# Folding the half sums of the exponentials for 14 pairs instead of 10, five of them with accumulating DMAs, and a drain behind every GpSimd addition

## The chip, the core and the metric

The kernel runs on one NeuronCore of a Trainium2 chip. The core has a matrix engine (TensorE, PE in the profile), VectorE (DVE), ScalarE (ACT), GpSimd (POOL), a queue engine that issues most of the DMAs (SyncE, SP), and 16 DMA engines that all the queues share. The metric is the device time of one launch in microseconds; the time before is the median of three runs.

## What is computed

The reference is an attention block followed by an MLP mixer, all in float32:

```python
B, H, S, D = 4, 8, 768, 64
mask = q_assign[:, :, :, None] == k_assign[:, :, None, :]   # nearest of 16 centroids
scores = np.where(mask, scale * q @ k.T, -1e9)
attn = np.exp(scores - max)
attn = attn / (attn.sum(-1) + 1e-9)
x = (attn @ v) laid out as (B, S, H*D)                      # 4 x 768 x 512
h = relu(x.T @ w_tok1) @ w_tok2                             # token mixing, 768 -> 256 -> 768
u = x + h.T
out = u + relu(u @ w_ch1) @ w_ch2                           # channel mixing, 512 -> 1536 -> 512
```

What the change touches is the row sum of the exponentials, `attn.sum(-1)`, which divides the product with `v`.

## The kernel before

**Stages.** The 32 heads are worked in 16 pairs (`NP`), `pair(m)` for m = 0 to 15. After them comes the token stage (`token1`, `token2`), then the channel stage, `channel1` and `channel2` for two groups of two batches each. The products of both MLP stages are done by a Strassen-like scheme with seven products instead of eight, so VectorE and GpSimd add and subtract operand blocks in between.

**A pair.** `scores(m)` makes the scores in 12 chunks on TensorE and ScalarE takes their exponential (L1193) into six buffers of 128 x 1536 floats, one for each block of 128 keys. `values(m, i)` multiplies block i with `v` (L1226), 16 matmuls a block. `add_up(m)` adds, on VectorE, the first three exponential buffers into `es[0]` (two additions) and the last three into `es[1]` (two additions); each is 128 x 1536. `sums(m)` multiplies them with a column of ones on TensorE, which sums over the partitions; it is issued one pair later, inside pair m+1, behind the first values block. `finish_x` transposes the result, takes the reciprocal and scales x.

**FOLD.** One character for each pair says how the two half sums are joined. With "-", `sums` runs TensorE over both `es` buffers, accumulating in PSUM. With "V", VectorE adds `es[0]` to `es[1]` first, and TensorE runs over `es[1]` alone. With "T", a DMA issued from GpSimd's queue adds `es[0]` to `es[1]` in SBUF while it moves it, and TensorE again runs over `es[1]` alone. The kernel before has "V" for pairs 1 to 10, "-" for pairs 0 and 11 to 15, and no "T".

```python
a, b = es[1], es[0]
if FOLD[m] == "V":
    tt(a.ap, a.ap, b.ap, ALU.add, 2 * S, a.k() + b.k(), a.k())
if FOLD[m] != "T":
    return
...
first = 0 if FOLD[m] == "-" else 1
for n in range(first, 2):
    mms(...)            # 4 matmuls of 384 columns, over es[n]
```

**Weight rounding.** Between these, VectorE rounds and recombines the MLP weights, in 31 pieces (`weight_round`, L1356 to L1374, five instructions a piece) with additions of 256 and 448 columns between them. The pieces start to be loaded at set times during the attention and are stored back to DRAM in the `wd` tensors.

**Order of the work.** The order on every engine but TensorE is made when the kernel is built: `Program.plan` is a list scheduler that knows a cost for each operation (the table `COST`, in us), latencies and due times, and puts each engine's instructions in the order that its model gives. The engines then run their queues strictly in that order and wait on semaphores. TensorE's order is the order in which the code issues the matmuls. A changed cost or operation can therefore move many instructions of VectorE, ScalarE, GpSimd and SyncE.

**Buffers.** There is one `es[0]` and one `es[1]`, used by every pair. VectorE cannot start `es[0]` of the next pair before whoever reads the old one is done.

**GpSimd.** It has 179 additions of 128 x 384 (`tt` with engine POOL, L883), all in the token and channel stages; most make the operand sums of the channel products, in two buffer sets that alternate from product to product.

Of the kernel before, what the change touches and what calls it, by code (L numbers as in the profile page):

```python
# [48 lines left out]
SUM_LO, SUM_HI = 1e-15, 1e15  # L49
GRAIN = 32  # L50
CHECK_AT = 532.0
FOLD = "-VVVVVVVVVV-----"

COST = {
    "ACT": (0.09, 0.00083),
    "ACT16": (-0.275, 0.001426),
    "JOIN16": (-0.165, 0.001426),
    "DVE": (0.075, 0.00104),
    "POOL": (0.12, 0.0023),
}  # L60
ISSUE = 0.63
BUS = 240e3
# [660 lines left out]
def kernel(  # L723
# [26 lines left out]
    nc = tc.nc  # L750
# [105 lines left out]
    def cost(kind, n):  # L856
        a, b = COST[kind]
        return a + b * n
# [22 lines left out]
    def tt(dst, a, b, op, n, rd, wr, engines=("DVE",)):  # L881
        def fn(e):
            (nc.vector if e == "DVE" else nc.gpsimd).tensor_tensor(out=dst, in0=a, in1=b, op=op)  # L883

        return g.add({e: cost(e, n) for e in engines}, fn, rd, wr)

# [184 lines left out]
    def route(m, bk):  # L1071
# [13 lines left out]
        def blocks(t):  # L1085
# [3 lines left out]
        vec(lambda: nc.vector.reduce_max(out=mxs.ap[:, 0:24], in_=blocks(a), axis=AX.X), 0.54,  # L1089
            a.k(), mxs.k())  # L1090
        tt(blocks(e), blocks(a), mxs.ap[:, 0:24].unsqueeze(2).to_broadcast([P, 24, C]),
           ALU.is_ge, HS, a.k() + mxs.k(), e.k())
        vec(lambda: nc.vector.transpose(out=o.ap, in_=e.ap), 0.56, e.k(), o.k())
# [107 lines left out]
    def add_up(m):  # L1201
        st = unit[m]
        for n in range(2):
            a = es[n]
            x, y, z = st[HJ * n : HJ * n + HJ]
            tt(a.ap, x.ap, y.ap, ALU.add, 2 * S, x.k() + y.k(), a.k())
            tt(a.ap, a.ap, z.ap, ALU.add, 2 * S, a.k() + z.k(), a.k())
# [6 lines that stand above are left out]
        def fn(e):  # L1214
            nc.gpsimd.dma_start(
                a.ap.rearrange("p h t -> p (h t)"), b.ap.rearrange("p h t -> p (h t)"),
                accum_op=ALU.add,
            )

        g.add({"POOL": 1.0}, fn, a.k() + b.k(), a.k(), (2.2 * 768 * 1024, 6144))  # L1220
# [30 lines left out]
    def sums(m, bk):  # L1251
        first = 0 if FOLD[m] == "-" else 1
        for n in range(first, 2):
            mms(
                [
                    (
                        ps[32 * gr : 32 * gr + 32, bk, 0:HS], ones.ap,
                        tokens(es[n].ap.rearrange("p h t -> p (h t)"), gr), n == first, n == 1,
                        (0, 32 * gr),
                    )  # L1260
                    for gr in range(4)
                ],
                0.645, es[n].k() + ones.k(), bank(bk), (P, 32),
            )
# [768 lines left out]
```

## Time and profile before

| | us |
|---|---|
| median of 3 runs | 793.61 (793.22 to 793.68) |
| profiled execution | 794.77 |
| its span | 793.0 |
| PE busy | 780.1 (98%) |
| VectorE busy | 677.5 (85%) |
| ScalarE busy | 461.2 (58%) |
| GpSimd busy | 190.2 (24%) |
| HBM traffic | 91.95 MB read, 28.61 MB written |

The span is the time from the first to the last instruction of the program; some 1.8 us of the profiled execution lie outside it. The granted TensorE clock was 0.999 of full speed. In the profile each float32 matmul is two records. The attention takes the span's first 329 us (the last matmul of L1226 starts at 329.0), the token stage runs to about 405, and the channel stage from there to 787.

### The profile page before, as it was taken

The numbers are of one execution on the slowest core, as the hardware profiler recorded it, in microseconds if no ns is written. First come the engines' busy times: TensorE is split into PE (matmuls) and PEld (weight loads), VectorE is DVE, ScalarE is ACT, GpSimd is POOL, SyncE is SP. The second block draws the span as 40 slices with busy tenths as digits, with TensorE's granted clock in tenths as the row PEclk, the third lists the DMA queues.
The fourth block names the chain that finished last, engine by engine and source line by source line (L and its number), as shares of the span: only waits on it lengthen the run. The fifth ranks groups of instructions, "written<-read, shape, count | busy, mean of one in ns | idle before, by whom it ended". The sixth has DMA issues, their size and how long they took to land.

```text
span 793.0 us, 15364 instructions
## 1 busy us (share of the span) xinstructions
PE 780.1 (98%) x5983; PEld 465.4 (59%) x5983; DVE 677.5 (85%) x876; ACT 461.2 (58%) x612; POOL 190.2 (24%) x185
## 2 busy tenths in 40 slices
PE   7999999999999999999999999999999999999997
PEld 6666666666666666544555555555555555555554
DVE  6869999999999999999999967899953567799964
ACT  4688898888898875599714367642245204400422
POOL 0000000000000000001264599700186379830000
PEclk9999999999999999999999999999999999999999
DMA  9576769777678953659858999975788844444767
GB/s 214 154 174 164 183 151 232 205 219 203 162 207 183 273 180 113 182 110 224 184 139 246 312 290 258 270 191 123 167 188 179 170 106 102 100 101 106 162 144 178
DMA packets 326576, 143.68 MB, mean 181 GB/s; under 512 B 260192, under 2 KB 322400, under 8 KB 326496
## 3 DMA queue, kind: packets, MB, share of 16 engines
q1 hardware_dynamic: 324128, 141.83, 71.4%
q8 instruction: 49, 0.80, 0.4%
q10 hardware_dynamic: 2368, 0.79, 0.4%
q14 instruction: 31, 0.25, 0.1%
HBM read 91.95 MB, written 28.61 MB: 152 GB/s over the span
## 4 chain that ended last, share of the span: by engine, by line
PE 88%; DVE 5%; ACT 3%; issue 2%; DMA 1%; SPq 0%; POOL 0%; DVEq 0%; POOLq 0%; ACTq 0%
PE ps L844 72%; PE ps L1226 16%; DVE arena L883 4%; ACT arena L873 2%; DMA wd<-arena 1%; ACT arena L1193 1%; DVE arena L865 0%; DVE arena L1360 0%; SPq L903 0%; DVE arena L1363 0%; ACT arena L863 0%; DVE arena L1366 0%; DVE arena L1356 0%; DVE arena L1280 0%; DVE arena L1273 0%
## 5 line engine op out<-in xcount | busy, mean ns | idle before, releaser
L844 PE MATMUL ps<-arena 128*128 128x384 f32 (+5 forms) x2735 | 642.4, 463 | 7.3 <-DVE arena L865 2.7
L844 PEld LDWEIGHTS ps<-arena 128*128 128x128 f32 (+1 forms) x2351 | 342.3, 185 | 252.8 <-issue 59.5
L883 DVE TENSOR_TENSOR arena<-arena 128x1536 f32<-128x1536 f32 (+6 forms) x350 | 370.2, 1079 | 10.5 <-PE ps L1226 2.3
L883 POOL TENSOR_TENSOR arena<-arena 128x384 f32<-128x384 f32 x179 | 189.5, 1094 | 510.8 <-DVE arena L883 379.4
L883 DVE TENSOR_TENSOR arena<-ps,arena 128x384 f32<-128x384 f32 (+3 forms) x227 | 189.6, 845 | 79.4 <-PE ps L844 75.4
L873 ACT COPY arena<-arena 128x768 uint16<-128x768 uint16 x221 | 189.4, 953 | 61.4 <-DMA arena<-arena 31.9
L1193 ACT ACTIVATE arena<-ps 128x768 f32<-128x768 f32 x192 | 150.6, 811 | 31.6 <-PE ps L844 29.9
L1226 PE MATMUL ps<-arena 128*32 128x192 f32 (+1 forms) x3248 | 144.7, 335 | 0.0
L1226 PEld LDWEIGHTS ps<-arena 128*32 128x32 f32 x3248 | 103.8, 110 | 44.0 <-issue 13.9
L863 ACT COPY arena<-ps 128x384 f32<-128x384 f32 (+2 forms) x41 | 29.5, 728 | 120.6 <-PE ps L844 120.4
L890 ACT ACTIVATE arena<-arena 128x1152 f32<-128x1152 f32 (+1 forms) x38 | 39.9, 1075 | 54.9 <-DVE arena L883 54.5
L1888 ACT ACTIVATE arena<-arena 128x768 f32<-128x768 f32 x40 | 38.7, 970 | 32.7 <-DMA arena<-in_moe_w_ch_dram 24.7
L844 PEld LDWEIGHTS <-arena 64*128 64x128 bf16 x384 | 19.3, 94 | 25.0 <-issue 0.6
L1360 DVE SCALAR_TENSOR_TENSOR arena<-arena 128x512 uint32<-128x512 uint32 (+1 forms) x31 | 20.6, 681 | 0.3
L1097 ACT ACTIVATE arena<-arena 128x384 bf16<-128x384 f32 x16 | 11.2, 703 | 16.1 <-issue 16.1
L1366 DVE SCALAR_TENSOR_TENSOR arena<-arena 128x512 f32<-128x512 uint32 (+1 forms) x31 | 20.2, 671 | 0.4
L1356 DVE TENSOR_SCALAR arena<-arena 128x512 uint32<-128x512 uint32 (+1 forms) x31 | 13.2, 435 | 5.8 <-DMA arena<-in_moe_w_tok_dram 5.8
L1273 DVE STREAM_TRANSPOSE arena<-ps 128x768 f32<-128x768 f32 x16 | 15.3, 955 | 0.0
L1363 DVE TENSOR_SCALAR arena<-arena 128x512 uint32<-128x512 uint32 (+1 forms) x31 | 14.4, 483 | 0.3
L865 DVE COPY arena<-ps 128x384 f32<-128x384 f32 (+3 forms) x12 | 8.0, 666 | 4.7 <-PE ps L844 4.6
L1088 DVE STREAM_TRANSPOSE arena<-ps 128x384 f32<-128x384 f32 x16 | 9.2, 575 | 3.1 <-PE ps L844 3.0
L1280 DVE STREAM_TRANSPOSE arena<-ps 128x384 f32<-128x384 f32 x16 | 9.3, 579 | 1.5 <-PE ps L1226 1.2
(58 smaller groups left out, 53.1 us busy)
## 6 DMA issues: line engine op xcount, KB each, us to landing
arena<-wd SPq DMA_DIRECT2D x196, 192.0 KB, 3.0
wd<-arena SPq DMA_DIRECT2D x84, 224.0 KB, 3.2
arena<-in_moe_w_ch_dram SPq DMA_DIRECT2D x96, 128.0 KB, 3.0
arena<-in_moe_w_ch_dram SPq DMA_DIRECT2D x16, 768.0 KB, 6.0
arena<-in_v_dram SPq DMA_DIRECT2D x16, 384.0 KB, 4.7
out_dram<-arena SPq DMA_DIRECT2D x14, 384.0 KB, 3.6
arena<-in_k_dram SPq DMA_DIRECT2D x13, 384.0 KB, 4.0
arena<-in_q_dram SPq DMA_DIRECT2D x13, 384.0 KB, 4.2
```

What stands on the lines that cost most here:

```text
L844: nc.tensor.matmul(dst, lhsT=lhsT, rhs=rhs, start=start, stop=stop, tile_position=pos, is_transpose=tr, skip_group_check=True,)
L863: nc.scalar.copy(out=dst, in_=src)
L873: nc.scalar.copy(out=dst, in_=src)
L883: (nc.vector if e == "DVE" else nc.gpsimd).tensor_tensor(out=dst, in0=a, in1=b, op=op)
L890: nc.scalar.activation(out=dst, in_=src, func=ACT.Relu)
L1193: lambda e, ex=ex, s=s, u=u: nc.scalar.activation(out=ex.ap[:, :, u * HS : (u + 1) * HS], in_=ps[:, 2 * s : 2 * s + 2, 0:HS], func=ACT.Exp ...
L1226: nc.tensor.matmul(dst, lhsT=lhsT, rhs=rhs, start=start, stop=stop, tile_position=pos, skip_group_check=True,)
L1273: lambda: nc.vector.transpose(out=x.ap[:, :, cols].rearrange("p j (c d) -> p c j d", d=32), in_=ps[:, 6:8, 0:HS],),
L1360: vec(lambda: nc.vector.scalar_tensor_tensor(out=TT, in0=hi, scalar=0xC0000000, in1=hh, op0=ALU.bitwise_and, op1=ALU.bitwise_or), 0.14 + 0 ...
L1363: vec(lambda: nc.vector.tensor_scalar(out=hh, in0=TT, scalar1=0xFF800000, scalar2=None, op0=ALU.bitwise_and), f, T.k(), h.k())
L1366: vec(lambda: nc.vector.scalar_tensor_tensor(out=ll, in0=lo, scalar=float(2.0**-52), in1=hh.bitcast(F32), op0=ALU.mult, op1=ALU.mult,), 0. ...
L1888: lambda e, i=i, func=func, bias=bias, n=n, hi=hi: nc.scalar.activation(out=hi, in_=hi, func=func, bias=bias, accum_out=wsum.ap[:, i, n : ...
```

## The change

Three edits. The string `FOLD` now folds pairs 1 to 14: VectorE does nine of them (1 to 5, 7, 9, 11, 13) and an accumulating DMA five (6, 8, 10, 12, 14). Every GpSimd addition is followed by a drain of GpSimd. And the scheduler's cost of a GpSimd addition gets 0.08 us more of fixed part.

```diff
-FOLD = "-VVVVVVVVVV-----"
+FOLD = "-VVVVVTVTVTVTVT-"
 COST = {
...
-    "POOL": (0.12, 0.0023),
+    "POOL": (0.2, 0.0023),
 }
...
     def tt(dst, a, b, op, n, rd, wr, engines=("DVE",)):
         def fn(e):
             (nc.vector if e == "DVE" else nc.gpsimd).tensor_tensor(out=dst, in0=a, in1=b, op=op)
+            if e == "POOL":
+                nc.gpsimd.drain()
```

The part of `add_up` that "T" reaches stood in the kernel before without being used:

```python
def fn(e):
    nc.gpsimd.dma_start(
        a.ap.rearrange("p h t -> p (h t)"), b.ap.rearrange("p h t -> p (h t)"),
        accum_op=ALU.add,
    )
g.add({"POOL": 1.0}, fn, a.k() + b.k(), a.k(), (2.2 * 768 * 1024, 6144))
```

Each such DMA moves 128 rows of 6144 bytes, 768 KB, from `es[0]` onto `es[1]`.

## The prediction

> **What bounds the kernel now.** The page first: the totals, the slices, the shares of the chain.
>
> ```profile
> PE 780.1 (98%) x5983; PEld 465.4 (59%) x5983; DVE 677.5 (85%) x876; ACT 461.2 (58%) x612; POOL 190.2 (24%) x185
> ...
> PE   7999999999999999999999999999999999999997
> ...
> DVE  6869999999999999999999967899953567799964
> ...
> PE 88%; DVE 5%; ACT 3%; issue 2%; DMA 1%; SPq 0%; POOL 0%; DVEq 0%; POOLq 0%; ACTq 0%
> ```
>
> TensorE sets the time nearly everywhere, so a matmul removed should be time removed. But VectorE is as full in the attention and in the token stage, so the next view is the chain of waits in order of time (start, duration, what).
>
> ```profile
> 230.87 9.89 PE ps L844 x72
> 240.76 5.98 PE ps L1226 x136
> 246.74 0.65 PE ps L844 x8
> 247.38 2.60 PE ps L1226 x64
> ...
> 299.88 9.23 PE ps L1226 x208
> ...
> 415.33 370.91 PE ps L844 x1154
> ```
>
> A pair is a scores block of 9.9 us and then values with sums, without a hole. The block at 240.76 holds a folded pair's sums: 200 records in 5.98 + 2.60 = 8.58 us. The one at 299.88 holds an unfolded pair's: 208 records in 9.23 us. Eight records more are 0.65 us. From 415 on the chain is TensorE alone. What lies between is seen in the busy time by stretch (PE, weight loads, VectorE, ScalarE, GpSimd, clock, DMA share, GB/s) and in TensorE's own timeline.
>
> ```profile
> 180.00:200.00 20.00, 20.00 (x288) 12.49 (x286) 19.23 (x26) 17.20 (x24) 0.00 (x0) 1.00 0.65 184
> 300.00:320.00 20.00, 20.00 (x308) 12.81 (x304) 19.68 (x28) 10.41 (x13) 0.00 (x0) 1.00 0.35 113
> 365.00:405.00 40.00, 39.33 (x115) 21.11 (x115) 38.59 (x78) 25.63 (x32) 11.83 (x12) 1.00 0.85 196
> 405.00:440.00 35.00, 34.64 (x108) 20.09 (x107) 33.08 (x38) 14.45 (x19) 19.86 (x18) 1.00 0.68 200
> 440.00:460.00 20.00, 20.00 (x64) 11.75 (x63) 17.08 (x19) 7.07 (x14) 12.08 (x13) 1.00 1.06 311
> ```
>
> ```profile
> 364.70 31.53 PE L844 MATMUL ps<-arena 128*128 128x384 f32 x91
> 396.73 18.24 PE L844 MATMUL ps<-arena 128*128 128x384 f32 x54 [0.50 <-DVE arena L883]
> 415.33 5.11 PE L844 MATMUL ps<-arena 128*128 128x384 f32 x15 [0.36 <-DVE arena L883]
> ```
>
> In the token stage VectorE is busy 38.59 of 40 us and TensorE waits for it: 91 records should take 91 x 0.3214 = 29.2 us (370.91 / 1154 is 0.3214), and took 31.53. So the end of the token stage is set by TensorE and VectorE together, and a gain of the attention reaches the end only if VectorE comes earlier too.
>
> **Part 1: matmuls removed.** Pairs 11 to 14 are folded anew. Each loses one pass of `sums`, 0.65 us by the two blocks above: 4 x 0.65 = 2.6 us, all on the path, since the blocks around it have no hole.
>
> **Part 2: VectorE's work.** Mean times of one instruction, by shape:
>
> ```profile
> L883 DVE TENSOR_TENSOR arena<-arena 128x1536 f32<-128x1536 f32 x90 | 156.4, 1747 | 5.4 <-PE ps L1226 2.3 <-ACT arena L1193 0.5 <-PE ps L844 0.2
> ...
> L883 DVE TENSOR_TENSOR arena<-arena 128x448 f32<-128x448 f32 x48 | 29.8, 634 | 0.0
> ...
> L883 DVE TENSOR_TENSOR arena<-arena 128x512 f32<-128x512 f32 x35 | 23.5, 686 | 1.9 <-DMA wd<-arena 1.5
> L883 DVE TENSOR_TENSOR arena<-arena 128x384 f32<-128x384 f32 x33 | 21.4, 663 | 0.7
> ...
> L1360 DVE SCALAR_TENSOR_TENSOR arena<-arena 128x512 uint32<-128x512 uint32 x27 | 18.5, 700 | 0.3
> L1366 DVE SCALAR_TENSOR_TENSOR arena<-arena 128x512 f32<-128x512 uint32 x27 | 18.1, 688 | 0.4
> ...
> L1363 DVE TENSOR_SCALAR arena<-arena 128x512 uint32<-128x512 uint32 x27 | 13.0, 502 | 0.3
> L1356 DVE TENSOR_SCALAR arena<-arena 128x512 uint32<-128x512 uint32 x27 | 11.7, 447 | 0.0
> ```
>
> Ten fold additions become nine: 1.75 us less. The scheduler also reorders. In the changed program's VectorE queue, the instructions that stand ahead of the last of the token stage's 56 evictions are fewer by that fold (1.75), four instructions of a rounding piece (0.45 + 0.50 + 0.69 + 0.69 = 2.33), five additions of 384 columns (5 x 0.66 = 3.3) and three of 448 (3 x 0.63 = 1.9): 9.3 us in all. Only 1.75 is gone; 7.5 us stand behind, in the channel stage's first 55 us, where VectorE was free for 1.9 of 35 and 2.9 of 20 us and freer later. I count them as hidden there by TensorE; if they come between the evictions instead, each can hold TensorE by some tenths, up to 2 us.
>
> **Part 3: the accumulating DMA, and what it makes wait.** No row of before shows one, nor any DMA issued by GpSimd. The nearest:
>
> ```profile
> arena<-in_moe_w_ch_dram SPq DMA_DIRECT2D x16, 768.0 KB, 6.0
> ...
> arena<-wdt SPq DMA_DIRECT2D x2, 768.0 KB, 5.1
> wdm<-arena SPq DMA_DIRECT2D x15, 96.0 KB, 2.1
> ```
>
> From below: it lands as the plain load of the same size, 5.1 us. From above: two busy loads one behind the other, 12.0 us. Between: the short DMA gives a fixed 2.1, so the data of 768 KB takes 3.0 to 3.9; an accumulation reads two sources, so 2.1 + 2 x 3.0 = 8.1 to 2.1 + 2 x 3.9 = 9.9. I take 8.8, nearer the quiet end, since the DMA share around pair 14 is 0.35.
>
> Two readers wait for it. TensorE's `sums(m)` come behind the rest of the pair's values and the next scores block, at least 9.9 + 2.6 = 12.5 us later by the chain's rows: covered. VectorE's next write of `es[0]` is the tight one. In the new queue it stands behind the routing and `finish_x`, which in before took from 190.97 to 195.43,
>
> ```profile
> 190.97 0.57 DVE L1088 STREAM_TRANSPOSE arena<-ps 128x384 f32<-128x384 f32 x1
> ...
> 195.43 0.76 DVE L1356 TENSOR_SCALAR arena<-arena 128x512 uint32<-128x512 uint32 x2
> ```
>
> 4.5 us, and then (pair 8) behind one L1360, one 448 addition, two L1363 and two L1366: 0.70 + 0.63 + 1.00 + 1.38 = 3.7. The cover is 8.2 us, near 8 for all five. At 8.8 VectorE waits 0.8 us a transfer, 4 us in all. Queued behind that write are rounding, the next half sums and the next pair's routing, which ScalarE waits for. A VectorE wait of this kind stands in before:
>
> ```profile
> DVE arena L883 <- DMA wd<-arena: 1.5, 1, 1.5
> ...
> 272.57 2.69 PE L844 MATMUL ps<-arena 64*128 64x384 f32 x18 [0.20 <-ACT arena L1193]
> ```
>
> VectorE stood 1.5 us for a DMA near 260, and TensorE lost 0.2 us to it at 272. So waits below some 1.5 us mostly die in slack: I price five at 0 to 0.2 each and take 0.5 together. By the token stage VectorE is still 9.3 - 4 = 5.3 us ahead of before, against TensorE's 2.6. TensorE's waits there (2.3 us of excess in the first row) should shrink; I take 0.5 back.
>
> The Trainium skill, "DMA: Bandwidth & Descriptors", section "Anatomy of one DMA — SWDGE (gpsimd) path", puts a DMA issued from GpSimd at 2.0 us plus its bytes over 436 GB/s, an estimate of 3.8 us for 768 KB; by it no wait would occur and the 0.5 would be saved. No run here shows it.
>
> **Part 4: the drains.** GpSimd's longest run:
>
> ```profile
> 639.95 38.33 POOL L883 TENSOR_TENSOR arena<-arena 128x384 f32<-128x384 f32 x40 [2.27 <-DVE arena L883]
> 679.19 1.00 POOL L883 TENSOR_TENSOR arena<-arena 128x384 f32<-128x384 f32 x1 [0.91 <-PE ps L844]
> 681.13 8.77 POOL L883 TENSOR_TENSOR arena<-arena 128x384 f32<-128x384 f32 x9 [0.93 <-PE ps L844]
> 690.87 10.73 POOL L883 TENSOR_TENSOR arena<-arena 128x384 f32<-128x384 f32 x6 [0.97 <-PE ps L844]
> ```
>
> An addition takes 1.00 alone and 0.96 in the run of 40: they overlap by 0.04, which a drain takes away at least. At most it costs another addition, 1.0. I take 0.1, near the low end, since it waits only for an addition that is ending: 56 x 0.1 = 5.6 us in this run. GpSimd's pauses here end when TensorE releases one of the two buffer sets, so it works about a product ahead: 7 x 3 matmuls x 2 records x 0.3214 = 13.5 us. Cost nothing; without that cover the lateness itself, 5.6 minus the pauses' 2.8, for each group.
>
> **The sum.** Against the profiled span: 793.0 - 2.6 + 0.5 - 0.5 = 790.4. The execution had 1.8 us more (794.77) and lies 1.2 above the median, so the median should fall from 793.6 to 791.0.
>
> **Rivals.** (a) *The accumulation outlasts its cover.* One mechanism: `es[0]` is held, VectorE stands five times, and the token stage ends when VectorE does. With a landing time L the waits are 5 x (L - 8). VectorE gives away the 2.6 us gain from 5 x (L - 8) = 9.3 - 2.6, L = 9.3, and the kernel is slower than before from L = 9.9. At L = 11 it is 15 - 9.3 = +5.7: 799.3; at 12, 804. For it: 9.9 is the busy end of my own estimate, and all this traffic shares 16 engines that are 0.65 busy. Against: the absorbed wait at 260.
>
> (b) *The issue itself is held up.* The Trainium skill, "SBUF — State Buffer", section "SBUF: two separate sides", says that VectorE instructions in a two-port mode lock GpSimd out of writing descriptors, so a DMA issued there starts late. As a mechanism here: the transfer starts only when VectorE leaves such instructions. Behind the issue stand 4.5 us of routing and `finish_x`; if the transfer began only behind half of them, L = 8.8 + 2.3 = 11.1 and the time is 799.8. Nothing in before can show it.
>
> (c) *The gain is caught in the reordering*: the 7.5 us put behind the token stage hold up evictions (2 us) and the waits cost another 0.5: 793.5, no change.
>
> (d) *Drains are dear.* From 56 d - 2.8 > 13.5, d = 0.29 us, TensorE waits in both groups; at d = 0.4 twice 6.1 us: 803. Against it: the drain has little left to wait for.
>
> (e) *Only the matmuls go and the token stage loses its waits*: with 2.0 of the 2.3 us of excess gone, 789.0.
>
> **Chances.** The forecast with (e) 0.60 (its own range 788.8 to 792.0), (c) 0.14, (a) 0.16, (b) 0.06, (d) 0.04. What a measurement of this kernel can tell from no change is about 0.2%, 1.6 us. So faster 0.60, same 0.14, slower 0.26. The range is 788.8 to 799.0: below it lies little, above it the longer half of (a) and (b), and (d).
>
> **What would show it.** Right: the values-and-sums blocks of pairs 12 to 15 at 0.65 us less each; VectorE idle before the 128x1536 additions under 1.5 us behind each transfer, released by a DMA; the last matmul of L1226 near 326.5 instead of 329; GpSimd's run at about 1.06 us an addition, with no TensorE wait on it. Wrong: landing times of the accumulating DMA above 9.3 us, VectorE idle by 2 us or more five times, TensorE's chain in the token stage broken by L883 for more than before, or TensorE waiting for GpSimd after 450.

## The result and the profile after

| | before | after |
|---|---|---|
| median, us | 793.64 | 813.96 |
| all executions, us | 793.22 to 793.87 (4) | 804.38, 806.09, 821.82, 838.73 |
| ratio | 1 | 1.0147 [1.0122, 1.0171] |
| profiled execution / its span, us | 794.77 / 793.0 | 806.09 / 804.3 |
| TensorE clock granted | 0.999 | 0.997 |

The change makes the kernel slower by 1.5%, 11.7 us of 793.6. The ratio rests on the executions of 804.38 and 806.09; the two longer ones, of which there is no profile, are left out of it. The profile is that of 806.09, 11.3 us above before's, so it shows what has to be explained. Where a part of the time is given below in us for a ratio, it is the ratio less 1, times 793.6.

The page of the changed kernel, the same lines as before and the queue of GpSimd's transfers (packets, MB, share of the 16 engines). From L885 on its lines have numbers two higher than before's: the sums and values are L1228, SyncE's transfers L905, its transposes L910.

```profile
PE 779.6 (97%) x5951; PEld 465.0 (58%) x5951; DVE 680.2 (85%) x875; ACT 460.5 (57%) x612; POOL 205.4 (26%) x190
...
PE   7999999999999879999999999989999999999996
...
DVE  6869999999999599999999977599973576689974
...
POOL 0000000000000000001264588820187268870000
...
q0 software_dynamic: 720, 3.93, 2.9%
...
PE 86%; DVE 9%; DMA 3%; issue 1%; ACT 0%; ACTq 0%; SPq 0%; DVEq 0%
```

TensorE has holes that it did not have: slices 14 and 15 (261 to 302 us) and slice 27 (523 to 543 us). GpSimd's first run of work now reaches into slice 27. VectorE has 9% of the chain instead of 5%, DMA 3% instead of 1%.

Comparing the two traces record by record of TensorE, in its order, gives where it fell back (us, negative is earlier than before):

| stretch of after | change there | running total |
|---|---|---|
| start of the program, to 21 | -1.0 | -1.0 |
| to 271, with the first of the missing passes | -1.2 | -2.2 |
| 272 to 297: pairs 12 and 13 | +8.0 | +5.8 |
| rest of the attention, two passes fewer | -1.1 | +4.7 |
| token stage | -0.9 | +3.8 |
| start of the channel stage, to 448 | +1.4 | +5.2 |
| 518 to 534: end of GpSimd's run, first group | +3.4 | +8.6 |
| 716 to 736: the same in the second group | +2.2 | +11.0 (0.2 elsewhere) |

The first row is hardly the change's: such a microsecond at the start comes and goes from run to run (e5 and e9 below have it, e3 and e6 have not). The last 0.3 us of the 11.3 lie behind TensorE's last records.

Three places carry it. The first, in the chain of waits of the changed kernel (start, duration, what), in its waits (who, for whom: us, times, longest) and in its stretches (columns as in the prediction; the first fence is the kernel before, the second the changed one):

```profile
258.77 2.13 PE ps L1228 x40
...
265.14 17.68 DMA arena<-arena
...
295.75 10.10 PE ps L844 x72
305.85 8.58 PE ps L1228 x200
```

```profile
DVE arena L883 <- DMA arena<-arena: 10.6, 4, 9.6
DVE arena L883 <- POOL arena L883: 4.3, 3, 2.0
PE ps L1228 <- DMA arena<-arena: 3.6, 1, 3.6
```

```profile
260.00:280.00 20.00, 19.80 (x288) 12.13 (x280) 18.36 (x28) 16.39 (x22) 0.00 (x0) 1.00 0.98 253
280.00:300.00 20.00, 20.00 (x295) 12.50 (x297) 18.96 (x30) 14.19 (x20) 0.00 (x0) 1.00 0.59 194
505.00:540.00 35.00, 35.00 (x110) 20.60 (x109) 33.11 (x36) 14.52 (x28) 5.53 (x4) 1.00 0.81 217
712.00:738.00 26.00, 26.00 (x83) 15.27 (x82) 25.65 (x27) 3.37 (x6) 0.00 (x0) 1.00 0.47 106
```

```profile
260.00:280.00 20.00, 19.32 (x288) 11.97 (x276) 12.43 (x21) 16.88 (x22) 0.86 (x1) 1.00 1.06 117
280.00:300.00 20.00, 13.93 (x208) 10.34 (x210) 16.74 (x21) 6.86 (x8) 0.00 (x0) 0.91 0.85 258
505.00:540.00 35.00, 32.29 (x99) 18.26 (x98) 27.07 (x27) 20.38 (x38) 21.94 (x15) 1.00 0.83 227
712.00:738.00 26.00, 24.32 (x75) 13.85 (x74) 24.64 (x24) 1.91 (x4) 7.03 (x4) 1.00 0.40 91
```

The accumulating transfer of pair 12, issued at 265.14, lands 17.68 us later. VectorE stands 9.6 us in front of `es[0]`, TensorE 3.6 us in front of `sums`, and is busy 13.93 of the 20 us from 280. The other three waits of VectorE for transfers are 1.0 us together (10.6 less 9.6). TensorE then stands 3.1 us more at 295.75, for VectorE's late routing. The two holes are 6.75 of the 8.0 us. Behind the first one the clock is granted at 0.50 for 3.4 us (from 284.1; the row from 280 shows the mean, 0.91), which is enough for the rest. From 260 to 280 the 16 DMA engines count as wholly busy (1.06) and yet move only 117 GB/s, where before's moved 253 at 0.98. SyncE's queue shows what else was issued just then, before (first fence) and after:

```profile
266.13 4.64 SPq L908 DMA_TRANSPOSE arena<-arena  x2
```

```profile
264.94 14.54 SPq L910 DMA_TRANSPOSE arena<-arena  x2
```

Issuing pair 12's two DMA transposes takes 14.54 us instead of 4.64. By the trace, they landed 17.9 and 17.5 us after their issue; in the kernel before, those of the attention's pairs take 3.7 to 6.1. The accumulating transfers of pairs 6, 8 and 12 are issued within 2 us of two transposes, that of pair 10 of one (the second is issued 7.9 us later); that of pair 14 has none beside it. All five, from the group of their source line:

```profile
DMA to landing us min/median/max: 5.7/8.1/17.7
```

The other two places are the ends of GpSimd's runs, third and fourth row of the stretches: TensorE is busy 32.29 of 35 and 24.32 of 26 us where it had no hole before. GpSimd's additions from 500 to 532 us, before and after, and VectorE's rows at the first place:

```profile
L883 POOL TENSOR_TENSOR arena<-arena 128x384 f32<-128x384 f32 x6 | 9.6, 1640 | 0.9 <-PE ps L844 0.9
```

```profile
L883 POOL TENSOR_TENSOR arena<-arena 128x384 f32<-128x384 f32 x19 | 26.5, 1394 | 3.1 <-issue 1.6 <-POOL arena L883 1.2 <-PE ps L844 0.4
```

```profile
522.92 3.43 DVE L883 TENSOR_TENSOR arena<-arena 128x1152 f32<-128x1152 f32 x2 [2.04 <-POOL arena L883]
526.28 0.54 DVE L883 TENSOR_TENSOR arena<-ps,arena 128x384 f32<-128x384 f32 x1
526.75 5.02 DVE L883 TENSOR_TENSOR arena<-arena 128x1152 f32<-128x1152 f32 x3
```

GpSimd's six last additions of before take 1640 ns in the mean, where one alone takes 1.00; single ones take 2.14. In the changed kernel 19 fall into these 32 us, and seven of them take 1.9 to 2.23 us. VectorE waits 2.04 us for GpSimd, and three of its additions of 1152 columns take 1.68 to 2.16 us instead of 1.35. TensorE waits behind them. The addition that starts second is the one that is longer:

```profile
510.26 1.35 DVE L883 TENSOR_TENSOR arena<-arena 128x1152 f32<-128x1152 f32 x1
```

```profile
510.34 2.13 POOL L883 TENSOR_TENSOR arena<-arena 128x384 f32<-128x384 f32 x1 [0.16 <-POOL arena L883]
```

### The profile page after: what moved, and what is told of

Its sections match the earlier page's. It is cut to its first block, busy times and chain, and to the rows that moved or that the text cites. A ratio compares the mean times of both kernels' runs of the same rounds, so it can differ in the third digit from the quotient of the medians.

```text
span 804.3 us, 15491 instructions
## 1 busy us (share of the span) xinstructions
PE 779.6 (97%) x5951; PEld 465.0 (58%) x5951; DVE 680.2 (85%) x875; ACT 460.5 (57%) x612; POOL 205.4 (26%) x190
## 4 chain that ended last, share of the span: by engine, by line
PE 86%; DVE 9%; DMA 3%; issue 1%; ACT 0%; ACTq 0%; SPq 0%; DVEq 0%
PE ps L844 71%; PE ps L1228 15%; DVE arena L883 7%; DMA arena<-arena 2%; DMA arena<-in_moe_w_ch_dram 0%; DVE arena L865 0%; DVE arena L1368 0%; DVE arena L1365 0%; ACTq L905 0%; ACT L984 0%; DVE arena L1090 0%; DVE arena L1282 0%; ACT arena L1195 0%; DVE arena L1362 0%; ACT arena L863 0%
## 5 line engine op out<-in xcount | busy, mean ns | idle before, releaser
L883 DVE TENSOR_TENSOR arena<-arena 128x1536 f32<-128x1536 f32 (+6 forms) x349 | 373.1, 1090 | 25.6 <-DMA arena<-arena 10.6
L883 POOL TENSOR_TENSOR arena<-arena 128x384 f32<-128x384 f32 x179 | 200.3, 1119 | 206.1 <-PE ps L844 97.0
L1228 PE MATMUL ps<-arena 128*32 128x192 f32 (+1 forms) x3216 | 144.1, 337 | 3.6 <-DMA arena<-arena 3.6
L1228 PEld LDWEIGHTS ps<-arena 128*32 128x32 f32 x3216 | 105.1, 111 | 45.7 <-issue 16.4
L1217 POOL DMA_DIRECT2D arena<-arena x5 | 4.4, 888 | 307.5 <-DVE arena L1282 307.5
L1358 DVE TENSOR_SCALAR arena<-arena 128x512 uint32<-128x512 uint32 (+1 forms) x31 | 12.6, 417 | 6.0 <-DMA wdm<-arena 6.0
L1099 ACT ACTIVATE arena<-arena 128x384 bf16<-128x384 f32 x16 | 11.3, 704 | 10.1 <-issue 10.0
L1365 DVE TENSOR_SCALAR arena<-arena 128x512 uint32<-128x512 uint32 (+1 forms) x31 | 12.9, 438 | 0.3
L1090 DVE STREAM_TRANSPOSE arena<-ps 128x384 f32<-128x384 f32 x16 | 9.2, 575 | 3.7 <-PE ps L844 3.7
```

The source lines that it names most:

```text
L1228: nc.tensor.matmul(dst, lhsT=lhsT, rhs=rhs, start=start, stop=stop, tile_position=pos, skip_group_check=True,)
L1365: vec(lambda: nc.vector.tensor_scalar(out=hh, in0=TT, scalar1=0xFF800000, scalar2=None, op0=ALU.bitwise_and), f, T.k(), h.k())
```

## The experiments

Times are medians, with the range of the executions and the ratio to the kernel before on the same chip, whose median was between 793.47 and 794.07 in all five sets.

| run | median (range), us | ratio [95%] |
|---|---|---|
| e1 folds alone | 808.07 (798.72 to 815.27) | 1.0207 [1.0158, 1.0256] |
| e2 drains and price | 801.42 (800.35 to 802.17) | 1.0089 [1.0072, 1.0106] |
| e3 no transfers | 799.43 (798.56 to 800.07) | 1.0066 [1.0049, 1.0083] |
| e4 transfers behind, in the plan | 839.40 (839.04 to 841.46) | 1.0580 [1.0562, 1.0597] |
| e5 price alone | 795.11 (794.34 to 796.22) | 1.0018 [1.0009, 1.0028] |
| e6 drains alone | 810.49 (809.21 to 811.86) | 1.0207 [1.0190, 1.0225] |
| e7 plain copies | 797.51 (797.12 to 798.78) | 1.0048 [1.0031, 1.0064] |
| e8 two late transfers | 800.12 (798.97 to 800.98) | 1.0086 [1.0069, 1.0103] |
| e9 the same, order held | 793.73 (793.24 to 795.32) | 0.9997 [0.9986, 1.0007] |
| e10 order held, pairs 11, 12 | 796.61 (795.08 to 797.67) | 1.0029 [1.0019, 1.0039] |
| e11 order held, three folds | 794.40 (793.20 to 796.56) | 1.0010 [0.9997, 1.0022] |
| e12 order held, VectorE only | 800.37 (799.18 to 800.63) | 1.0070 [1.0050, 1.0090] |
| e13 transposes moved away | 803.37 (802.23 to 804.43) | 1.0116 [1.0099, 1.0133] |
| e14 order held, five transfers | 798.75 (798.28 to 801.39) | 1.0073 [1.0052, 1.0093] |
| e15 the same as copies | 795.50 (795.17 to 797.64) | 1.0029 [1.0016, 1.0041] |
| e16 the same, transposes moved | 802.41 (801.50 to 802.75) | 1.0107 [1.0090, 1.0124] |
| e17 all but pair 12's | 800.81 (797.52 to 807.52) | 1.0114 [1.0063, 1.0166] |
| e18 pair 12's alone | 799.79 (798.04 to 801.11) | 1.0068 [1.0043, 1.0092] |

### The change taken apart: e1 to e4

The theories behind the expectations: the transfers collide with the DMA transposes (A); the drains cost the time and the spread (B); any accumulating transfer costs VectorE its landing (C); the drains cost nothing (D); the reordered SyncE queue alone makes the transposes slow (E); an accumulating transfer disturbs every DMA (F).

**e1**, the kernel before with the new folds alone:

```diff
-FOLD = "-VVVVVVVVVV-----"
+FOLD = "-VVVVVTVTVTVTVT-"
```

> Only the FOLD string is changed; no drains, old cost of a GpSimd addition. Theory A (two separate losses: the accumulating transfer of pair 12 ran at the same time as two DMA transposes and all three took 17 us, 8.7 us of TensorE time; the drains cost some 5.6 us in the channel stage): the channel stage is as before, the collision stays a matter of luck, so some runs near 791 to 793 and others up to 30 us more; the executions differ by 5 us or more among themselves. Rival B (the drains are behind the spread and the loss): tight runs at 791. Rival C (the transfers always cost VectorE their landing time): tight runs at 797 or more, with VectorE waiting behind all five.

Measured 798.72 to 815.27. The spread is there without a drain, so B falls. In the profiled execution (798.72, the shortest of the four) all transfers landed within 8.2 us and VectorE waited 0.7 us for them in all: no collision of 17 us. Its loss lay somewhere that none of the theories had: by 412 us TensorE was 4.7 us ahead of before (0.8 of it from the start of the program), and between 440 and 516 us it lost 8.1, beside GpSimd's additions. TensorE's timeline there,

```profile
509.93 10.31 PE L844 MATMUL ps<-arena 128*128 128x384 f32 x26 [4.72 <-DVE arena L883]
```

and VectorE's just ahead of it:

```profile
506.17 5.84 DVE L883 TENSOR_TENSOR arena<-arena 128x1152 f32<-128x1152 f32 x3
```

Three additions of 1152 columns in a row take 1.95 us each here, while GpSimd is adding, where before three in a row took 4.02 us behind GpSimd's run, 1.34 each:

```profile
516.25 4.02 DVE L883 TENSOR_TENSOR arena<-arena 128x1152 f32<-128x1152 f32 x3
```

That is a cost of the new order of VectorE's work, and e8 and e9 follow it up.

**e2**, before with the drains and the scheduler's new price, old folds:

```diff
-    "POOL": (0.12, 0.0023),
+    "POOL": (0.2, 0.0023),
...
+            if e == "POOL":
+                nc.gpsimd.drain()
```

> The drains and the new cost, with the old FOLD (ten folds by VectorE, no transfer). Theory A: no spread (under 1 us among the executions), 793.6 + 5.6 = 799, with GpSimd's additions 0.2 us farther apart and the loss where VectorE's combinations of the second channel product meet GpSimd's late additions. Rival D (the drains cost nothing, what was lost in the channel stage came from the late token stage or from the attention): 793 to 794.

801.42, with 1.8 us between the executions: 7.1 us more, so D falls. TensorE loses 4 us at 515 to 524 and 2.5 at 716 to 733, the changed kernel's second and third place.

**e3**, the changed kernel without its five transfers (those pairs are not folded):

```diff
-FOLD = "-VVVVVTVTVTVTVT-"
+FOLD = "-VVVVV-V-V-V-V--"
```

> The changed kernel with its five transfers taken away: pairs 6, 8, 10, 12, 14 are not folded, so TensorE has 5 x 0.65 = 3.2 us more to do than in the changed kernel. Theory A: 799 + 0.65 = 799.7, no spread: under 1 us. Rival E (the reordered SyncE queue, not the transfers, makes the transposes slow): executions still differ by 5 us or more, transposes near 17 us still seen.

799.43, within 1.5 us. Without transfers no spread and no long transposes. Its SyncE order is not quite the changed kernel's, since the scheduler plans it without transfers; e7 below has that order itself, and no spread either, so E falls.

**e4** meant to put each transfer behind the transposes, by naming their buffers among its inputs to the scheduler:

```diff
-        g.add({"POOL": 1.0}, fn, a.k() + b.k(), a.k(), (2.2 * 768 * 1024, 6144))
+        tr = qkt[0].k() + qkt[1].k()
+        g.add({"POOL": 1.0}, fn, a.k() + b.k() + tr, a.k(), (2.2 * 768 * 1024, 6144))
```

> The changed kernel, with each transfer waiting until the two DMA transposes issued before it have landed. Theory A: transposes land in 4 to 6 us again, transfers in 6 to 8 us, no spread; the attention is 2.6 us shorter than before and the drains cost 5.6 us: 796.6, plus up to 2 us where VectorE waits for a transfer that now starts later. Rival F (an accumulating transfer disturbs whatever else the DMA engines carry): spread and long landings stay.

839.4, and it tells nothing of A against F: such names steer only the scheduler's order, and on the chip the transfer (149.87) still started before the transposes (150.31 and 153.59). The order got much worse: TensorE waits 32.5 us for VectorE's routing. Inconclusive; e13 does it properly.

### Drains and price apart: e5, e6

```diff
-    "POOL": (0.12, 0.0023),
+    "POOL": (0.2, 0.0023),
```

> The kernel before with the planner's price of a GpSimd addition at 0.2 + 0.0023 n instead of 0.12 (the change's value) and nothing else: no drains, the old folds, no accumulating transfer. Both changes of GpSimd together made 801.42 against 793.99. If the drains themselves cost it (0.16 us an addition), this kernel is at 793 to 795. If the new order that the price brings costs it, it is at 798 to 802 and TensorE loses its time at the same two places, 515 to 525 and 716 to 733 us.

```diff
+            if e == "POOL":
+                nc.gpsimd.drain()
```

> The kernel before with a drain behind each GpSimd addition, the planner's price left at 0.12, the old folds. If the drains cost it: 799 to 803, with GpSimd's run of additions ending about 58 x 0.2 = 11 us later than before's 510 and VectorE's wide combinations lengthened by it. If only the price's order costs it: 793 to 795.

The new order costs 1.4 us, the drains in the old order 16.4. Both together cost 7.1: the price is what makes the drains bearable. e6 is far above the 799 to 803 expected. GpSimd with drains (e6, its own timeline), then TensorE:

```profile
498.46 1.00 POOL L883 TENSOR_TENSOR arena<-arena 128x384 f32<-128x384 f32 x1 [0.16 <-issue]
499.62 1.01 POOL L883 TENSOR_TENSOR arena<-arena 128x384 f32<-128x384 f32 x1 [0.16 <-issue]
```

```profile
479.70 25.00 PE L844 MATMUL ps<-arena 128*128 128x384 f32 x77
510.87 9.53 PE L844 MATMUL ps<-arena 128*128 128x384 f32 x21 [6.17 <-POOL arena L883]
```

One addition now starts 1.16 us after the other, with 0.16 idle, instead of the 0.96 of before: 0.20 us each. TensorE stands 6.17 us for the 81st of GpSimd's 179 additions, which ends at 509.89. In the kernel before the same addition is the last of this row:

```profile
493.08 6.86 POOL L883 TENSOR_TENSOR arena<-arena 128x384 f32<-128x384 f32 x7 [0.93 <-PE ps L844]
```

It ended at 499.94, and the matmul that stands in e6 started at 504.44 there. In e6 this matmul starts 0.98 us after the addition's end, so GpSimd was 3.5 us ahead in before; now it is 9.9 us late. The second group reads the same: the addition ended at 689.90, its matmul started at 694.42, and in e6 TensorE stands 5.58 us. Behind both holes the clock is granted at 0.50 for 6.8 us, which costs most of the other 5 of the 17 us that TensorE loses in this trace. The waits of before do not tell this. They count four waits of VectorE for GpSimd,

```profile
DVE arena L883 <- POOL arena L883: 2.4, 4, 0.6
```

but VectorE waits 0.58 us for TensorE's products before and after these, and its additions start 0.1 us after TensorE's product there, as the one at 493.11 does, which is put down to TensorE.

### Accumulation or copy: e7

The changed kernel with the same five transfers as plain copies; order and queues stay. Five pairs' denominators lack one of their halves.

```diff
             nc.gpsimd.dma_start(
                 a.ap.rearrange("p h t -> p (h t)"), b.ap.rearrange("p h t -> p (h t)"),
-                accum_op=ALU.add,
             )
```

> The changed kernel with the five GpSimd transfers as plain copies of the same size to the same place, no addition in them (five pairs' denominators then lack one of their two halves). Theory 1, the reading and adding in the accumulating transfer is what runs into the DMA transposes: packets fall from 478 ns towards 240 ns, the five land in 3.5 to 6 us, no landing over 10 us, and the time is that without transfers, 799 to 801, with runs within 2 us. Theory 2, any transfer from GpSimd's queue beside the transposes collides: landings up to 17 us again, and runs spread over more than 5 us up to 820 and more.

797.51, within 1.7 us. The five landed in

```profile
DMA to landing us min/median/max: 3.5/5.5/6.9
```

and a packet of 6144 bytes took 234 to 240 ns, against 478 when accumulating. Only the accumulation differs from the change, so it costs 7.9 us here (11.7 less 3.8). It is not harmless either: beside the copy of pair 12 the two transposes took 7.27 us to issue, against 4.64 before. Theory 1 holds; the time came out a little below its 799 to 801. In the two profiles TensorE's records of the changed kernel and of e7 are 0.5 us apart at 270, 9.2 at 300 and 7.1 at the end: nearly all of the difference lies where pair 12's transfer took 17.7 us.

### A pair of transfers without transposes, and the order: e8, e9

e8 is the kernel before with two more folds, by transfers in pairs 13 and 14, where no transposes are issued.

```diff
-FOLD = "-VVVVVVVVVV-----"
+FOLD = "-VVVVVVVVVV--TT-"
```

> The kernel before with two more pairs folded, 13 and 14, both by accumulating transfers ("-VVVVVVVVVV--TT-"), no drains, price 0.12. In these two pairs no DMA transposes are issued any more. Theory A (only the meeting with transposes hurts): both land in 5.2 to 6.5 us, VectorE waits under 1.5 us for them, two passes of the sums go (2 x 0.65 = 1.3 us), runs agree within 2 us, and the time is 792 to 793.5. Theory C (an accumulating transfer always costs VectorE its landing): 795 or more, with VectorE waiting 3 us or more for each. If the reordering of VectorE's later work matters more than the transfers: 795 to 800, with the loss behind 440 us.

Theory A's part on the transfers was right: no reader waited for them. But the time was 800.12, all of the loss behind 440 us. VectorE's groups from 455 to 500 us in e8, and the timeline of TensorE:

```profile
L883 DVE TENSOR_TENSOR arena<-ps,arena 128x1152 f32<-128x1152 f32 x23 | 31.2, 1355 | 10.0 <-PE ps L844 9.8
L883 DVE TENSOR_TENSOR arena<-arena 128x448 f32<-128x448 f32 x4 | 3.6, 928 | 0.0
L883 DVE TENSOR_TENSOR arena<-arena 128x256 f32<-128x256 f32 x2 | 1.7, 868 | 0.0
```

```profile
450.55 15.75 PE L844 MATMUL ps<-arena 128*128 128x384 f32 x48 [0.63 <-DVE arena L883]
466.77 39.52 PE L844 MATMUL ps<-arena 128*128 128x384 f32 x120 [0.47 <-POOL arena L883]
508.32 4.11 PE L844 MATMUL ps<-arena 128*128 128x384 f32 x12 [2.03 <-DMA arena<-wd]
513.76 6.69 PE L844 MATMUL ps<-arena 128*128 128x384 f32 x20 [1.33 <-DVE arena L883]
```

In the kernel before, VectorE had only evictions in this stretch. In e8 the additions of 448 and 256 columns stand between them, with both inputs in SBUF, and last 928 and 868 ns in the mean, where they have means of 634 and 434 over the whole of before; GpSimd runs at the same time. Three of the six take 1.2 to 1.28 us and the others no more than usual. The evictions, which have one input in PSUM, stay at 1355.

e9 holds the order: the scheduler plans the kernel before, and the folds are added as its order is written out.

```diff
+        def fold():
+            if FOLD[m] == "V":
+                nc.vector.tensor_tensor(out=a.ap, in0=a.ap, in1=b.ap, op=ALU.add)
+            if FOLD[m] == "T":
+                nc.gpsimd.dma_start(a..., b..., accum_op=ALU.add)
...
+        if PLAN[m] == "V":
+            tt(a.ap, a.ap, b.ap, ALU.add, 2 * S, a.k() + b.k(), a.k()).fn = lambda e: fold()
+        else:
+            last = o.fn
+            o.fn = lambda e: (last(e), fold())
```

`PLAN` is the old string, `o` the last addition of `es[1]`, and `sums` writes no matmuls for the missing pass.

> The same two transfers as in e8 (pairs 13 and 14, no drains), but the planner plans the kernel before and the folds are put in as its order is written out: every other instruction of VectorE, ScalarE, GpSimd and SyncE stands where it stood before, and of TensorE only the two passes of the sums are missing. Theory R (e8's 6.4 us came from the new order, which puts VectorE's additions on on-chip data into GpSimd's time): 792 to 793, two passes of 0.65 below the 793.7, no VectorE additions of 256 or 448 columns between 455 and 500 us, runs within 2 us. If the transfers themselves or TensorE's being earlier cost it: 797 to 801 as in e8.

793.73, ratio 0.9997: the 6.8 us of e8 are gone, with the same transfers held in before's order. TensorE through the same stretch:

```profile
439.73 80.47 PE L844 MATMUL ps<-arena 128*128 128x384 f32 x249
```

Theory R holds in that the order costs the 6.8 us. How much of it the longer additions make is not shown: in e8 the six are 2.1 us longer together, and TensorE also waits 2.03 us for a load. The two passes' 1.3 us are not seen in the time (interval -1.1 to +0.6 us). The profiled span of 791.6 is 1.4 below before's, but 1.0 of that is the start of the program.

### Where the transfers lie: e10, with e11 and e12

As e9, with `FOLD` `"-VVVVVVVVVVTT---"`, `"-VVVVVVVVVV-VTT-"` and `"-VVVVVVVVVVVVVV-"`.

> As e9, the order of before held, but the two transfers in pairs 11 and 12, in which two DMA transposes each are issued, instead of 13 and 14. Theory A (an accumulating transfer and transposes slow each other): landings of the transfers 7 us and more and of the transposes 6 us and more in these two pairs, VectorE waits 2 us or more for one of them at least, runs spread over more than 2 us, median 794 to 805. If the place does not matter: 792 to 793 like e9.

796.61, 2.3 us (1.5 to 3.1) above before, where e9 is level with it; the two transfers are the same, two pairs earlier. The transfer of pair 11 met its transposes (landings 6.2 and 8.9 us); that of pair 12 was issued at 275.6, behind them. The loss did not come by `es[0]`: no reader waited for the transfers themselves. It came by SyncE's queue:

```profile
246.23 6.83 SPq L908 DMA_TRANSPOSE arena<-arena  x2
```

```profile
263.00 3.42 DVE L883 TENSOR_TENSOR arena<-arena 128x512 f32<-128x512 f32 x4 [4.01 <-DMA wd<-arena]
```

```profile
270.77 11.65 PE L844 MATMUL ps<-arena 64*128 64x384 f32 x72 [2.64 <-DVE arena L1088]
```

Issuing the transposes takes 6.83 us (4.83 in e9, from 245.94), the five stores to `wd` behind them are issued from 256.32 instead of 252.99, VectorE stands 4.01 us for the buffer of a store, and TensorE 2.64 us for the routing behind that. TensorE's 2.64 us are followed by 3.4 us of a clock granted at 0.50. A's sign is right; the spread and the size expected were too large for it.

> As e9, the order held, with pair 12 folded by VectorE besides (one more addition of 1.75 us): three passes of the sums go, 1.95 us. If VectorE has room there: 791.5 to 792.5, below both kernels. If its 1.75 us is carried to the end of the token stage: 793 to 794.

794.40: neither gain nor loss beyond the interval.

> The order of before held, no transfers and no drains, pairs 11 to 14 folded by VectorE: four passes go (2.6 us) and VectorE gets 4 x 1.75 = 7.0 us more ahead of the token stage, where TensorE waited 2.3 us for it in all. If VectorE's work is carried over in full: 793.7 + 7.0 - 2.6 = 798 at most. If the attention hides it: 791. Which of the two it is says what a transfer that takes VectorE's addition is worth at all.

800.37, above the full carry of 798: in this part VectorE's addition of 1.75 us costs its whole time and more, for 0.65 us of TensorE.

### The meeting itself: e13 to e18

e13 is the changed kernel with the transposes of four pairs moved in SyncE's queue, as the order is written out; the other queues are untouched.

```diff
+        for t in [o for o, _ in order if o.acc]:
+            for p in [o for o, _ in order if o.more and abs(o.end - t.end) < 6]:
+                at = [o for o, _ in order].index(p)
+                pair = order.pop(at)
+                while order[at][0].end < t.end + 8 and order[at][0] not in p.succs:
+                    at += 1
+                order.insert(at, pair)
```

> The changed kernel, with one thing moved: in the four pairs that have both, the two DMA transposes stand about 8 us of the plan later in SyncE's queue, behind the accumulating transfer instead of beside it; every other queue is the same instruction by instruction. Theory A (the meeting with transposes is what costs): the five transfers land in 5 to 6.5 us, no landing of either kind over 10 us, runs within 4 us, median 797 to 801, near the 797.5 of plain copies. If the accumulation as such is slow and disturbs any DMA: landings above 7 us and a spread over 10 us stay, median 805 and more.

803.37, within 2.2 us: the spread is gone, no landing reaches 9 us, and VectorE waits 0.8 us for transfers in all. But the transfers still land after 5.7 to 8.5 us, where A said 5 to 6.5, and the median is above the 797 to 801 of A. The chain shows a new way, around pair 6:

```profile
152.21 8.11 DMA arena<-in_k_dram
160.33 7.56 DMA arena<-arena
167.92 3.83 ACT arena L882 x4
```

A load of k that runs beside the transfer takes 8.11 us (such loads have a median of 4.1 in this run), the transposes start when it has landed (they wait for a semaphore that it releases), and ScalarE's copies behind them (L882) hold TensorE. So the experiment brought a cost of its own, and it shows that the transfer slows a load as well, a point for F. In four executions of each, the spread is gone with the meetings. How much of the 7.9 us the meetings cost in the executions without a profile is not shown.

> The five transfers and four VectorE folds of the change put into the order of before as in e9 (held), no drains. Four passes of the sums go (2.6 us). Theory A: the transfers of pairs 6, 8, 10 and 12 meet transposes, landings 7 to 18 us, a wait of VectorE of several us in pair 12, runs spread over more than 5 us, median 797 to 810. If drains and order were all: 790.5 to 792.

> As e14, with the five transfers as plain copies (five pairs' denominators lack one half). Landings 3 to 6.5 us as in e7, no spread: 791 to 793 if what is left is only four passes less of TensorE and one addition less of VectorE. The difference to e14 is the price of accumulating.

> As e14, with the transposes of the four pairs moved about 8 us later in SyncE's queue as in e13. Theory A: 791 to 794, runs within 3 us, transfers landing in 5 to 6.5 us. If it does not help: as e14.

With the order held and no drains (`FOLD` as in the change; e15 without `accum_op`, e16 with e13's move): 798.75, 795.50 and 802.41. Accumulating costs 3.5 us beside copies here (5.8 less 2.3). The copies alone miss their 791 to 793, though four passes are gone; the change gives VectorE two additions more in pairs 11 and 13, and e12 shows what such additions cost in this order, but that they make the whole of it is not shown. VectorE waits for transfers twice in e14, 5.3 us, and three times in e16, 6.1 us, with landings of 8.6 at most: the cover of 8 us belongs to the changed kernel's order. Moving the transposes (e16) makes it worse, as in e13, because they come late: TensorE waits 3.7 us for L882. In e14 the late starter was again pair 12's transfer, at 276.68 and so behind its transposes; three met theirs and landed within 8.4 us. No kernel with five transfers came down to before.

The last two take transfers out of the changed kernel one way and the other; VectorE folds in the places where the transfers were issued.

```diff
+            if m == 12:     # e18: m != 12
+                nc.vector.tensor_tensor(out=a.ap, in0=a.ap, in1=b.ap, op=ALU.add)
+                return
```

> The changed kernel, with the fold of pair 12 done by VectorE in the place where the transfer was issued; the other four transfers and every queue's order stay. If the spread comes from pair 12's transfer alone: runs within 4 us, median 799 to 803 (e7's 797.5 with copies, the other four meetings at up to 1 us each, one addition of 1.75 us more for VectorE). If it can come from each meeting with transposes: the spread over 10 us stays, median 806 and more.

> The changed kernel with the transfer of pair 12 alone; the folds of pairs 6, 8, 10 and 14 are done by VectorE in the places where their transfers were issued. If pair 12's transfer alone makes the spread: runs from about 804 to over 815 us, and a landing over 12 us in the profile. If it needs the other transfers too: runs within 4 us, 800 to 806 (four additions of 1.75 us more for VectorE than in e17's kind).

e17 spreads from 797.52 to 807.52 with a median between its two expectations, e18 only from 798.04 to 801.11. So in four executions each pair 12's transfer alone does not make the spread, and it can come without it. Its landing in e18 was 8.0 us, though it met transposes that landed after 6.1 and 9.0.

## Why the prediction was wrong

Two steps failed: in Part 3 the one landing time for all five transfers, and in Part 4 the cover of the drains.

**Part 1, the matmuls: right.** The block at 305.85 is 8.58 us for 200 records, 0.65 below the unfolded 9.23, as predicted. Where no transfer took long, the whole attention and token stage came out as forecast: at 412 us TensorE is 3.9, 3.4 and 3.1 us earlier in the profiles of e1, e7 and e17 than in before, the start of the program left out, against 2.6 and 0.5. The 2.3 us of excess that the 0.5 was taken from were read too high: six of the 91 records have 512 columns and take 0.43 us each, 0.6 us more together.

**Part 3, the transfers: right for four of the five, wrong for one, and that one cost most.** The landing was taken as 8.8 for all five, between 5.1 and 12.0; its median is 8.1. The cover of about 8 us was right too: three waits, 1.0 us together, and 17.7 less 9.6 is 8.1 at the fourth. The step that failed is the one landing time with its upper bound of 12.0, worked out from plain loads: the prediction weighed only the share of busy DMA engines. Before's own SyncE queue issues two DMA transposes 1.5 us apart in each of the pairs 6, 8, 10 and 12. In the profiled execution the transfer and the transposes of pair 12 were slow together, 17.7 us, and with that rival (a)'s mechanism ran: `es[0]` held, VectorE standing 9.6 us. It ran once there and not five times, and some 7 of its 8.0 us reached the end. e7 shows that accumulating is what it takes (7.9 us less with copies). No kernel whose transfers, accumulating or transposes beside them are taken away spreads by more than 2.5 us (e3, e7, e13, e15, e16). It takes more than a meeting: e14 and e18 meet transposes too and spread by 3.1 us. Rival (b), an issue held up by VectorE, is not borne out. Where no transposes were issued beside them (pairs 13 and 14 of e9), the first packets went 1.4 to 1.6 us after the issue, though VectorE's additions and routing ran on. Beside transposes they went after 1.7 to 4.0 us in the changed kernel, but pair 12's after 2.3, so its 17.7 us are no late start. By the Trainium skill ("DMA: Bandwidth & Descriptors", section "Anatomy of one DMA — SWDGE (gpsimd) path": 2.0 us plus bytes over 436 GB/s) the estimate was 3.8 us. The fastest plain copy landed after 3.5, no accumulating transfer before 5.7.

**Part 4, the drains: wrong in size by two, and in its cover.** A drain was taken as 0.1 us and is 0.20. That alone would have changed nothing, since the prediction's threshold was 0.29: it counted 13.5 us of cover, a product that GpSimd is ahead of TensorE. That step failed: e6 shows 3.5 us in both groups. The pauses that the prediction read lie where GpSimd waits for a buffer; the matmuls that need its last sums soonest were not looked for. So the mechanism of rival (d) came at 0.20 instead of 0.29, lighter in the change than in e6 since the scheduler's new price moved work: 7.1 us with it (e2) against 16.4. Two things more were not in the prediction: additions of VectorE and GpSimd hold each other up where GpSimd's run meets those of 1152 columns (in before already, longer in the changed kernel), and the clock falls behind a hole of TensorE.

**Part 2, VectorE's order: "hidden there by TensorE" holds only by a margin.** The changed kernel lost 1.4 us at the start of the channel stage, within the 2 us allowed. But such a reordering can cost far more: e8 against e9 shows 6.8 us for nothing else. Additions with both inputs in SBUF were counted at their mean over the whole kernel, and in e8 were put beside GpSimd's additions. The Trainium skill, "SBUF — State Buffer", section "Who interferes with whom", says that a VectorE instruction with two inputs in SBUF contends with a GpSimd instruction that reads SBUF, and one with at most one such input does not, outside the two-port modes. The traces agree: e8's additions of 448 columns take 928 ns there, its evictions 1355 as always. They also show that it need not cost VectorE anything: in the same stretch the mean of four such additions is 616 ns in e1 and 670 in the changed kernel.

**The sum.** From the runs, in us: four passes -2.6, drains with price +7.1 (e2), accumulating instead of copying +7.9 (after against e7): +12.4, against +11.7 measured. The last term is measured against e7, so what is tested is e7 alone: -2.6 + 7.1 = 4.5 against 3.8 [2.5, 5.1]. That it closes is in part luck, for the terms do not simply add, since each edit gives another order. e3 should have 7.1 + 0.65 = 7.8 and has 5.2 [3.9, 6.5]; the folds alone (e1) and the drains alone (e6) cost 16.4 each, more than the whole change.

**What stays open.** Why one meeting of a transfer with transposes lasts 8 us and another 17.7 in nearly the same places. The packets show only that the DMA engines stood together: thirteen of the transfer's packets that began at 273.7 all ended at 277.9, 4.2 us later. Open is also what the longer executions of the changed kernel, of e1 and of e17 consist of, since each kernel has one profile, and those of e1 and e17 are of their shortest.

## What to carry to other kernels

Before giving an off-path engine more to do, find the instruction that needs its results soonest and read how far ahead they are: 3.5 us here, which 0.20 us on each of some 50 additions used up almost three times over. Pauses of the engine elsewhere do not show it. Before adding a transfer, list what the other queues issue in the same microseconds, and count what stands behind in those queues. A scheduler's order can be worth more than the edit: hold the old order and add the edit alone, and the two are told apart.

## What the runs showed of the hardware

- An accumulating transfer of 768 KB within on-chip memory: 478 ns for a packet of 6144 bytes against 234 for a copied one; 5.7 us at the least to its landing, 3.5 for the copy. Beside two DMA transposes mostly 7.6 to 8.4 us, once 17.7; the transposes then take mostly 5 to 10, once 17.9, instead of 3.7 to 6.1. With none issued beside it, it still took up to 8.6 (e13, e16).
- A DMA transpose occupies its issuing queue while it is slowed: 14.54 us for two against 4.64, and everything behind is late.
- A drain behind each GpSimd addition of 128 x 384 costs 0.20 us: 1.16 from one to the next against 0.96.
- VectorE and GpSimd additions that both read SBUF lengthen each other, the one that starts second: 448 columns from 0.61 to 1.28 us, 1152 columns from 1.35 to 2.16, GpSimd's 384 columns from 1.00 to 2.23. Evictions from PSUM are not touched (1.355 us).
- Behind a wait of TensorE of 2.64 us (e10), 3.64 (after) and 4.72 (e1) the clock was granted at 0.50 for 3.4 us, behind 5.58 and 6.17 us (e6) for 6.8. Not every such wait did it: behind the changed kernel's second one, of 3.11 us, it stayed at 1.00.
